# Attention and a gated MLP on one core: a sixth W1 buffer, other loads of k, q and v, and scale vectors spread by VectorE

## The chip, the cores and the metric

The kernel runs on one core of a Trainium2 chip. The metric is the device time of one execution in microseconds (us), as the median of several runs. The core has a matrix engine (TensorE, PE in the profile; its weight loads are shown apart as PEld), a vector engine (VectorE, DVE), an activation engine (ScalarE, ACT), a general engine (GpSimd, POOL) and an engine that here only issues transfers (SyncE, SP). Each takes its own instructions in order and waits for the others on semaphores.

## The reference

For each of 8 batches there is grouped-query attention (16 query heads, 4 key/value heads, 384 positions, head size 64). Its output, as 384 x 1024 values `x`, goes through a residual block that mixes positions and then a residual MLP of width 4096.

```python
k = np.repeat(k, 4, axis=1); v = np.repeat(v, 4, axis=1)
scores = (1 / 8) * np.matmul(q, k.transpose(0, 1, 3, 2))
attn = np.exp(scores - max); attn = attn / attn.sum(-1)
x = np.matmul(attn, v)                  # heads side by side: 384 x 1024
a1 = alpha1 * x + beta1
tok = np.einsum('ts,bsd->btd', w_tok, a1)
u = x + lam * tok
a2 = alpha2 * u + beta2
ch = np.maximum(a2 @ w_ch1, 0.0) @ w_ch2
out = u + lam * ch
```

All inputs are float32 in HBM; the matrix products run in bf16. The vectors `alpha1`, `beta1`, `alpha2`, `beta2` and `lam` have 1024 entries, one for each model column.

## The kernel before

**Passes.** `main(b)` is the MLP of batch b, in two passes. The first pass makes the 32 hidden blocks (`nt`, 128 rows of W1 columns each): 8 matmuls of 384 columns for each block, line L414, into one of two PSUM banks (tag "mm"). Even blocks are moved out of PSUM by ScalarE (L422), odd ones by VectorE (L424), so the bank of an odd block must be emptied while the next even block is computed. The second pass makes the output from the resident W2, 6 groups of 32 matmuls of 512 columns, L447. W1 does not stay: it comes as 16 chunks of two blocks for every batch, by GpSimd's casting loads (`load_w1`, L134), into a ring of `RING` buffers; a buffer's next load is issued when PE has finished the chunk in it. W2 comes once, in 16 pieces (`load_w2`, L139), in the first batch's passes.

**Side work.** `side(b + 1)` is the attention and position mixing of the next batch, written in small pieces between the matmuls of `main(b)`. `main` yields after every half block; a dictionary gives the pieces that follow each yield. `us[0]` are the units of the first pass, `us[1]` those of the second. In the first batch the blocks 0 to 3 are made early, so the units 0 to 3 are their ends, and from unit 4 on a unit divisible by four lies in the middle of an even block. All five engines' orders are as written (`manual_schedule`); an engine never passes over an instruction that waits.

**The lead.** Batch 0 has no pass before it: `side(0)` runs alone, about the first 37 us. Its order is `add(scores, i)` for 18 groups, with the dictionary `at` giving what follows each: the transposes of k and q, `av`, `a1`, `tok` and `spread`. Each `scores` group fills a PSUM pair that ScalarE empties with one exponential (L226).

**The scale vectors.** `vecs` holds four vectors on all 128 partitions: `g1` = alpha1, `h1` = beta1 times lam, `al2` = alpha2, `lam_t` = lam. They start as rows of float32 in 32 partitions (`rows_f`); `split` cuts them into three bf16 parts (L532, L534, L540), and `spread` (L332, L334) sends them to all partitions by matmuls with a selection matrix, followed by a copy from PSUM. `g1` is spread in the lead (after the score groups 3 and 12); the other three are spread in the first batch's first pass, at the units 34 to 54.

**k, q and v.** k of batch b comes as two float32 loads on SP's queue (`load_k`, L96, two staging buffers `kst`) and is cast and doubled by four copies (`place_k`, L107): for batch 2 on, by GpSimd. q and v come by GpSimd's casting loads (L116, L111). `load_next(b + 2)` issues these four copies, four q loads and three v loads. For batch 2 it stands at the end of the first batch's first pass, for later batches in the second pass. k and q are turned by TensorE (`k_transpose`, `q_transpose`) for batches 0 and 1 and by DMA transposes on SP's queue (`flip_k`, `flip_q`) from batch 3 on; of batch 2, k and the first quarter of q go by DMA transpose, the other three quarters of q by TensorE at the units 16, 24 and 32 of batch 1's first pass.

Of the kernel before, what the change touches and what calls it, by code (L numbers as in the profile page):

```python
# [12 lines left out]
def kernel(  # L13
# [21 lines left out]
    nc = tc.nc  # L35
# [13 lines left out]
    P = 128  # L49
# [8 lines left out]
    RING = 5  # L58
# [16 lines left out]
    hT = const.tile([P, NNT, S], bf, tag="hT", name="hT")  # L75
    vecs = const.tile([P, 4, DM], f32, tag="vecs", name="vecs")
# [3 lines left out]
    kT = const.tile([P, NST, Hkv, P], bf, tag="kT", name="kT")  # L80
# [10 lines left out]

    def load_k(b, hs=(0, 2)):
        ks.setdefault(b, [])
        for h in hs:
            t = sb.tile([P, 2, NST, D], f32, tag="kst", name="kst", bufs=2)
            nc.sync.dma_start(out=t, in_=k[b, h:h + 2].rearrange("h (p st) d -> p h st d", st=NST))  # L96
            ks[b].append(t)

    def place_k(b, i, hs=(0, 1)):
        if b not in k2s:  # L100
            k2s[b] = sb.tile([P, NST, Hkv, 2, D], bf, tag="k2", name="k2", bufs=1)
        copies = [nc.gpsimd.tensor_copy] * 2
        if b == 1 or b == 0 == i:
            copies = (nc.vector.tensor_copy, nc.vector.tensor_copy if i else nc.scalar.copy)
        lo, hi = hs[0], hs[-1] + 1
        for a in range(2):
            copies[a](out=k2s[b][:, :, 2 * i + lo:2 * i + hi, a, :], in_=ks[b][i][:, lo:hi].rearrange("p h st d -> p st h d"))  # L107
# [5 lines left out]
    def load_q(b):  # L113
        qrs[b] = sb.tile([P, Hq, NST, D], bf, tag="q_raw", name="q_raw", bufs=1)
        for h in range(0, Hq, G):
            nc.gpsimd.dma_start(out=qrs[b][:, h:h + G], in_=q[b, h:h + G].rearrange("h (p st) d -> p h st d", st=NST))  # L116

    def flip_k(b):
        nc.sync.dma_start_transpose(out=kT.rearrange("p st h s -> p (st h) s"),
                                    in_=k2s[b].rearrange("p st h a d -> p (st h a d)"))  # L120
# [53 lines left out]
    def side(b):  # L174
# [14 lines left out]
        def k_transpose(h0, n=2, tag="tp"):  # L189
            ps = tp_ps([P, n * NST, P], tag)  # L190
            for i in range(n * NST):
                nc.tensor.matmul(out=ps[:, i, :], lhsT=k2s[b][:, i % NST, h0 + i // NST].rearrange("p a d -> p (a d)"),
                                 rhs=ident, is_transpose=True, start=(i == 0), stop=(i == n * NST - 1), skip_group_check=True)
            nc.vector.tensor_copy(out=kT[:, :, h0:h0 + n, :].rearrange("p st h s -> p h st s"),
                                  in_=ps.rearrange("p (h st) s -> p h st s", h=n))
# [13 lines left out]
        def scores(i, later=False):  # L209
            sc = bank([P, 2, 4, P], "sc", "sc") if first else three()  # L210
            k = 4 * i
            while k < 4 * i + 4:
                n = min(4 * i + 4, k - k % NST + NST) - k
                p, sk, st = k // (NST * NST), k // NST % NST, k % NST
                for hh in range(2):
                    r = slice(hh * D, (hh + 1) * D)
                    nc.tensor.matmul(out=sc[:, hh, k % 4:k % 4 + n], lhsT=kT[r, sk, 2 * p // G, :],  # L217
# [109 lines left out]
        def spread(ps_, vs, tag, eng="DVE"):  # L327
            n = len(ps_)
            ps = bank([P, 4, P], tag, "vec")
            w = vs[1] - vs[0]  # L330
            for i, p in enumerate(ps_):
                nc.tensor.matmul(out=ps[:, i * w:(i + 1) * w], lhsT=sel[:, p:p + 1].to_broadcast([P, P]),  # L332
                                 rhs=rows_b[:, vs[0] * P:vs[1] * P], start=True, stop=True)
            evac(eng)(out=vecs[:, vs[0]:vs[1], ps_[0] * P:(ps_[-1] + 1) * P].rearrange("p v (n d) -> p n v d", n=n),  # L334
                      in_=ps[:, :n * w].rearrange("p (n v) d -> p n v d", n=n))
# [16 lines left out]
        if not first:  # L352


            turns = {16 + 8 * i: [(q_transpose, 2 + 2 * i, 2, "three")] for i in range(3)} if b == 2 else {}
            if b == 1:
                turns = {4: [(split, 2, 4, 0)], 8: [(split, 2, 4, 1)], 12: [(k_transpose, 0)],
                         16: [(q_transpose, 0, 2, "av")], 20: [(k_transpose, 2)]}
                for i in range(3):
                    turns[24 + 4 * i] = [(q_transpose, 2 + 2 * i, 2, "av")]  # L360
                for i in range(4):
                    turns[34 + 4 * i] = [(spread, (2 * i, 2 * i + 1), (1, 3), "tp", "ACT")]
                for i in range(2):
                    turns[50 + 4 * i] = [(spread, range(4 * i, 4 * i + 4), (3, 4), "av", "ACT")]
# [13 lines left out]
              2: [(q_transpose, 2, 2, "av")], 3: [(warmup, 1), (spread, lower, (0, 1), "tp")],  # L378
              4: [(av, 0)], 5: [(a1, 0)], 6: [(av, 1), (k_transpose, 2, 2, "tp")],
# [3 lines left out]
              12: [(spread, upper, (0, 1), "av"), (a1, 2)], 13: [(tok, 0), (av, 4), (a1, 3)],  # L383
# [12 lines left out]
    def load_next(b):  # L396
        place_k(b, 0)
        place_k(b, 1)
# [4 lines left out]
    def main(b):  # L403
# [3 lines left out]
        for c in range(NCH):  # L407
# [27 lines left out]
            if b == 0 and c == NCH - 1:  # L435
                for i in range(RING):
                    load_w1(NCH + i)
                load_next(2)
# [20 lines left out]
    with tc.manual_schedule(engines=order):  # L459
# [11 lines left out]
        hTf = hT.rearrange("p n s -> p (n s)")  # L471
# [25 lines left out]
        load_row(2, moe_alpha2)  # L497
# [44 lines left out]

        def fill_h(p):
# [17 lines left out]
        load_k(1)  # L561
# [4 lines left out]
        for f in side(0):  # L566
            f()
        place_k(1, 0)
        place_k(1, 1)
        load_k(2)  # L570
        for b in range(B):
            us = side(b + 1) if b + 1 < B else ({}, {})
            moves = [(0, 1, flip_k, 2), (0, 1, flip_q, 2, 0, 2)] if b == 1 else []
            if 0 < b < B - 2:
                moves += [(1, 1, load_k, b + 2), (1, 2, load_next, b + 2), (1, 34, flip_k, b + 2), (1, 36, flip_q, b + 2, 0, 2),
# [39 lines left out]
```

The softmax here doesn't subtract the row's maximum and nothing guards it: scores larger than these inputs give would overflow.

## Time and profile before

| what | value |
|---|---|
| median of 5 runs | 803.92 us (803.0 to 804.14) |
| profiled execution: its own time | 803.92 us |
| profiled execution: span of the program's instructions | 802.1 us |
| PE busy | 794.8 us, 99% of the span |
| DVE, ACT, POOL busy | 344.7, 226.5, 181.9 us |
| granted TensorE clock | 1.00 |
| one first pass, from batch 2 on | about 41.6 us |
| one second pass | about 55.0 us |
| DMA moved | 112.58 MB, mean 140 GB/s |

The profile is that of one execution. The span runs from the first to the last instruction of the program; 1.8 us of the execution's time lie outside it. A busy PE is not necessarily a PE at its peak, since matmuls are pipelined and their ends are modelled; the distance from one matmul's start to the next tells more.

### The profile page before, as it was taken

The numbers are of one execution on the slowest core, as the hardware profiler recorded it, in microseconds if no ns is written. First come the engines' busy times: TensorE is split into PE (matmuls) and PEld (weight loads), VectorE is DVE, ScalarE is ACT, GpSimd is POOL, SyncE is SP. The second block draws the span as 40 slices with busy tenths as digits, with TensorE's granted clock in tenths as the row PEclk, the third lists the DMA queues.
The fourth block names the chain that finished last, engine by engine and source line by source line (L and its number), as shares of the span: only waits on it lengthen the run. The fifth ranks groups of instructions, "written<-read, shape, count | busy, mean of one in ns | idle before, by whom it ended". The sixth has DMA issues, their size and how long they took to land.

```text
span 802.1 us, 14253 instructions
## 1 busy us (share of the span) xinstructions
PE 794.8 (99%) x6141; PEld 453.7 (57%) x6141; DVE 344.7 (43%) x667; ACT 226.5 (28%) x308; POOL 181.9 (23%) x241
## 2 busy tenths in 40 slices
PE   8999999999999999999999999999999999999997
PEld 4765555655556555565555655566555655556545
DVE  7652565316542256323662235622365225552122
ACT  7624331232412243123221234122431223312100
POOL 9234231341013500135002340033300330003000
PEclk9999999999999999999999999999999999999999
DMA  9999999999279962999339991499914994139611
GB/s 190 203 194 202 204 207 161 193 197 133 63 139 181 198 95 62 171 190 195 64 84 162 193 192 42 96 172 198 162 47 114 174 196 83 47 65 183 83 40 40
DMA packets 232575, 112.58 MB, mean 140 GB/s; under 512 B 81976, under 2 KB 226368, under 8 KB 232512
## 3 DMA queue, kind: packets, MB, share of 16 engines
q0 software_dynamic: 170752, 83.47, 79.0%
q1 hardware_dynamic: 61216, 27.81, 13.8%
q8 instruction: 48, 0.79, 0.4%
q10 hardware_dynamic: 544, 0.39, 0.2%
q14 instruction: 15, 0.12, 0.0%
HBM read 170.53 MB, written 12.58 MB: 228 GB/s over the span
## 4 chain that ended last, share of the span: by engine, by line
PE 86%; DMA 9%; issue 3%; DVE 1%; POOL 1%; ACT 0%; POOLq 0%
PE ch L447 37%; PE h L414 36%; DMA w<-in_moe_w_ch_dram 9%; PE sc L217 4%; PE sc L252 3%; PE sc L275 3%; POOL w L134 1%; PE h L168 1%; PE tok L275 0%; PE av L252 0%; PE warm L464 0%; PE tp L203 0%; PE ut L292 0%; DVE hT L534 0%; PE tok L279 0%
## 5 line engine op out<-in xcount | busy, mean ns | idle before, releaser
L447 PE MATMUL ch<-w,hT 128*128 128x512 bf16 (+2 forms) x1600 | 357.6, 371 | 0.9 <-DVE o L452 0.9
L414 PE MATMUL h<-a2T,w 128*128 128x384 bf16 (+1 forms) x2016 | 331.9, 326 | 0.2 <-DMA w<-in_moe_w_ch_dram 0.2
L414 PEld LDWEIGHTS <-w 128*128 128x128 bf16 x2016 | 196.5, 98 | 130.3 <-DMA w<-in_moe_w_ch_dram 1.4
L134 POOL DMA_DIRECT2D w<-in_moe_w_ch_dram x128 | 112.2, 877 | 525.7 <-PE h L414 507.0
L447 PEld LDWEIGHTS <-hT 128*128 128x128 bf16 x1600 | 144.7, 98 | 152.6 <-issue 10.1
L226 ACT ACTIVATE es<-sc 128x1024 bf16<-128x1024 f32 x126 | 121.4, 1023 | 187.7 <-PE sc L217 178.8
L424 DVE TENSOR_SCALAR hT<-h,bias 128x384 bf16<-128x384 f32 x128 | 79.1, 618 | 215.7 <-PE h L414 215.1
L422 ACT ACTIVATE hT<-h,bias 128x384 bf16<-128x384 f32 x128 | 74.3, 580 | 304.4 <-PE h L414 303.8
L452 DVE TENSOR_TENSOR o<-ch,vecs 128x512 f32<-128x512 f32 (+2 forms) x50 | 33.4, 669 | 107.9 <-PE ch L447 107.9
L252 PEld LDWEIGHTS <-es 128*128 128x128 bf16 x1008 | 38.3, 97 | 13.2
L275 PEld LDWEIGHTS <-wtokT 128*128 128x128 bf16 x576 | 37.4, 98 | 12.3 <-DVE a L265 1.7
L217 PE MATMUL sc<-qT,kT 64*128 64x384 bf16 (+2 forms) x576 | 42.1, 272 | 0.2
L252 PE MATMUL sc<-v,es 128*128 128x65 bf16 x1008 | 39.8, 193 | 0.0
L257 DVE RECIPROCAL rinv<-sc 128x6 f32<-128x6 f32 x56 | 10.8, 192 | 67.3 <-PE sc L252 66.7
L282 DVE TENSOR_TENSOR x<-sc,x 128x384 f32<-128x384 f32 x56 | 30.9, 552 | 20.0 <-PE sc L275 20.0
L275 PE MATMUL sc<-a,wtokT 128*128 128x128 bf16 x504 | 37.3, 219 | 0.0
L217 PEld LDWEIGHTS <-kT 64*128 64x128 bf16 x576 | 21.6, 94 | 24.0 <-issue 18.6
L453 DVE TENSOR_TENSOR o<-o,x 128x512 f32<-128x512 f32 (+2 forms) x50 | 33.5, 670 | 1.7
L286 DVE TENSOR_TENSOR a<-x,vecs 128x384 bf16<-128x384 f32 x56 | 32.6, 582 | 1.9
L263 DVE TENSOR_TENSOR a1f<-x,vecs 128x384 f32<-128x384 f32 x56 | 31.2, 557 | 1.9
L265 DVE TENSOR_TENSOR a<-a1f,vecs 128x384 bf16<-128x384 f32 x56 | 31.2, 557 | 1.9
L258 DVE TENSOR_TENSOR x<-sc,rinv 128x384 f32<-128x384 f32 x56 | 31.2, 557 | 1.9
(80 smaller groups left out, 211.8 us busy)
## 6 DMA issues: line engine op xcount, KB each, us to landing
w<-in_moe_w_ch_dram POOLq DMA_DIRECT2D x144, 512.0 KB, 8.9
out_dram<-o SPq DMA_DIRECT2D x47, 256.0 KB, 2.2
q_raw<-in_q_dram POOLq DMA_DIRECT2D x28, 192.0 KB, 8.6
kst<-in_k_dram SPq DMA_DIRECT2D x16, 192.0 KB, 3.7
v<-in_v_dram POOLq DMA_DIRECT2D x24, 64.0 KB, 8.3
a2T<-a SPq DMA_TRANSPOSE x56, 2.3
qg<-in_q_dram POOLq DMA_DIRECT2D x3, 192.0 KB, 4.6
stage<-in_q_dram ACTq DMA_DIRECT2D x2, 192.0 KB, 3.6
```

Source lines behind the costliest of these rows:

```text
L134: nc.gpsimd.dma_start(out=t, in_=w1src[:, :, c * CW * P:(c + 1) * CW * P])
L217: nc.tensor.matmul(out=sc[:, hh, k % 4:k % 4 + n], lhsT=kT[r, sk, 2 * p // G, :], rhs=qT[r, p, st:st + n, :], start=True, stop=True)
L226: nc.scalar.activation(out=e, in_=sc, func=EXP, scale=scale_qk)
L252: nc.tensor.matmul(out=av[:, hh, sq, :], lhsT=ess[k // 4][:, m % 2, k % 4, :], rhs=vb[:, sk, hk, :], start=(sk == 0), stop=(sk == NST - 1))
L275: nc.tensor.matmul(out=ps[:, tt, :], lhsT=wtokT[:, st, tt * P:(tt + 1) * P], rhs=a1s[p][:, st, :], start=(st == 0), stop=(st == NST - 1 an ...
L286: nc.vector.tensor_tensor(out=a2s[p], in0=u, in1=bc(al2, p), op=MUL)
L414: nc.tensor.matmul(out=ps[:, :n], lhsT=w1[:, dt, j * P:(j + 1) * P], rhs=a2T[:, dt, :n], start=(dt == 0), stop=(dt == NDT - 1))
L422: nc.scalar.activation(out=hT[:, nt, :], in_=ps[:, :S], func=RELU, bias=c1)
L424: nc.vector.tensor_scalar(out=hT[:, nt, :], in0=ps[:, :S], scalar1=c1, scalar2=0.0, op0=ADD, op1=mybir.AluOpType.max)
L447: nc.tensor.matmul(out=ps[:, lo:hi], lhsT=hT[:, nt, ms * P:(ms + 1) * P], rhs=w2[:, nt, dw * 512 + lo:dw * 512 + hi], start=(nt == 0), sto ...
L452: nc.vector.tensor_tensor(out=o[:, lo:hi], in0=ps[:, lo:hi], in1=lam_t[:, c], op=MUL)
L453: nc.vector.tensor_tensor(out=o[:, lo:hi], in0=o[:, lo:hi], in1=x[:, ms, c], op=ADD)
```

## The change

`RING` goes from 5 to 6, and the two pieces of code that depend on it move with it: the prologue loads six W1 chunks before q and v of batch 1, and the W2 loads of the first pass start one chunk earlier.

k of batch 2 and later comes by two casting loads on GpSimd's queue, straight into `k2` in both copies; SP's loads, the staging buffers and GpSimd's copies for these batches are gone. k of batches 0 and 1 is still staged, in a free part of `hT`. `k2` and `kT` have another layout, with the table `BLK` telling which block holds which third of the positions; the number and size of the matmuls stay.

At the end of the first batch's first pass only k of batch 2 is loaded. Its q is loaded in four pieces after the chunks 1 to 4 of batch 1's first pass, and its v after chunk 10. All four quarters of this q are turned by TensorE, at the units 24, 32, 40 and 48.

`spread` is left for `g1` alone, and its first half stands after score group 5 instead of 3. The other three vectors are loaded as rows of 512 entries into partitions 0, 32, 64 and 96 of three tiles (cleared by GpSimd first), and one VectorE stream shuffle for each half sends partition 0 of each group of 32 to the whole group. Two shuffles stand at each of the units 4, 12 and 20 of the first batch's first pass, each pair after the other's rows are loaded anew; `h1` is made by one product at unit 16. The transposes of batch 1 move to the units 8 and 24 to 40. k of batch 1 is loaded after the fourth piece of `side(0)`.

```diff
-    RING = 5
+    RING = 6
...
     def load_k(b, hs=(0, 2)):
+        if b > 1:
+            k_tile(b)
+            for a in range(2):
+                nc.gpsimd.dma_start(out=k2s[b][:, :, a], in_=by_head(k[b]))
+            return
         for h in hs:
-            t = sb.tile([P, 2, NST, D], f32, tag="kst", name="kst", bufs=2)
-            nc.sync.dma_start(out=t, in_=k[b, h:h + 2].rearrange("h (p st) d -> p h st d", st=NST))
+            ks[b, h // 2] = t = hTf[:, 7680 + 384 * h:8448 + 384 * h].bitcast(f32).rearrange(
+                "p (h st d) -> p h st d", h=2, st=NST)
+            nc.sync.dma_start(out=t, in_=by_head(k[b, h:h + 2]))
...
-            turns = {16 + 8 * i: [(q_transpose, 2 + 2 * i, 2, "three")] for i in range(3)} if b == 2 else {}
+            turns = {24 + 8 * i: [(q_transpose, 2 * i, 2, "three")] for i in range(4)} if b == 2 else {}
             if b == 1:
-                turns = {4: [(split, 2, 4, 0)], 8: [(split, 2, 4, 1)], 12: [(k_transpose, 0)],
-                         16: [(q_transpose, 0, 2, "av")], 20: [(k_transpose, 2)]}
+                turns = {4: [(to_all, 3, 0, 0), (to_all, 3, 1, 1), (load_row_set, 1, 1, 0), (load_row_set, 2, 0, 1)],
+                         8: [(k_transpose, 0)], 12: [(to_all, 1, 0, 2), (to_all, 1, 1, 0), (load_row_set, 2, 1, 0)],
+                         16: [(scale_beta,)], 20: [(to_all, 2, 0, 1), (to_all, 2, 1, 0)],
+                         24: [(q_transpose, 0, 2, "av")], 28: [(k_transpose, 2)]}
                 for i in range(3):
-                    turns[24 + 4 * i] = [(q_transpose, 2 + 2 * i, 2, "av")]
-                for i in range(4):
-                    turns[34 + 4 * i] = [(spread, (2 * i, 2 * i + 1), (1, 3), "tp", "ACT")]
-                for i in range(2):
-                    turns[50 + 4 * i] = [(spread, range(4 * i, 4 * i + 4), (3, 4), "av", "ACT")]
+                    turns[32 + 4 * i] = [(q_transpose, 2 + 2 * i, 2, "av")]
...
-              2: [(q_transpose, 2, 2, "av")], 3: [(warmup, 1), (spread, lower, (0, 1), "tp")],
-              4: [(av, 0)], 5: [(a1, 0)], 6: [(av, 1), (k_transpose, 2, 2, "tp")],
+              2: [(q_transpose, 2, 2, "av")], 3: [(warmup, 1)],
+              4: [(av, 0)], 5: [(spread, lower, "tp"), (a1, 0)], 6: [(av, 1), (k_transpose, 2, 2, "tp")],
...
     def load_next(b):
-        place_k(b, 0)
-        place_k(b, 1)
+        load_k(b)
...
             if b == 0 and c == NCH - 1:
                 for i in range(RING):
                     load_w1(NCH + i)
-                load_next(2)
+                load_k(2)
+            if b == 1 and c in range(1, 5):
+                load_q(2, [G * (c - 1)])
+            if b == 1 and c == NCH - RING:
+                load_v(2)
...
+        def load_row_set(i, half, place):
+            ap = (moe_alpha1, moe_beta1, moe_alpha2, moe_lam)[i]
+            nc.sync.dma_start(out=rows4[place][0:P:32],
+                              in_=bass.AP(tensor=ap.tensor, offset=ap.offset + half * 512, ap=[[0, 4], [1, 512]]))
+
+        def to_all(i, half, place):
+            nc.vector.stream_shuffle(out=vecs[:, i, half * 512:(half + 1) * 512], in_=rows4[place], mask=[0] * 32)
+
+        def scale_beta():
+            nc.vector.tensor_tensor(out=h1, in0=h1, in1=lam_t, op=MUL)
...
-        load_k(1)
         load_q(1)
         load_v(1)
         for i in range(3):
             load_w2(0, i, 8)
-        for f in side(0):
+        for i, f in enumerate(side(0)):
             f()
+            if i == 3:
+                load_k(1)
+        for i in range(3):
+            rows4.append(sb.tile([P, 512], f32, tag="es", name="rows4", bufs=EB))
+            nc.gpsimd.memset(rows4[i], 0.0)
+            load_row_set(*((3, 0), (3, 1), (1, 0))[i], i)
         place_k(1, 0)
         place_k(1, 1)
-        load_k(2)
...
-            moves = [(0, 1, flip_k, 2), (0, 1, flip_q, 2, 0, 2)] if b == 1 else []
+            moves = [(0, 1, flip_k, 2)] if b == 1 else []
             if 0 < b < B - 2:
-                moves += [(1, 1, load_k, b + 2), (1, 2, load_next, b + 2), (1, 34, flip_k, b + 2), (1, 36, flip_q, b + 2, 0, 2),
+                moves += [(1, 2, load_next, b + 2), (1, 34, flip_k, b + 2), (1, 36, flip_q, b + 2, 0, 2),
```

## The prediction

> **What bounds the kernel now.** I read the page's slices first, then the waits of PE, then the table by pass, and last the timelines of the two places that the change touches.
>
> ```profile
> PE   8999999999999999999999999999999999999997
> PEclk9999999999999999999999999999999999999999
> DMA  9999999999279962999339991499914994139611
> ```
>
> PE is busy in every slice at a full granted clock; the DMA engines are full only up to about 190 us and then in each first pass. The waits of PE (total us, times, longest):
>
> ```profile
> PE vec L332 <- DVE hT L540: 0.8, 1, 0.8
> PE h L414 <- DMA w<-in_moe_w_ch_dram: 0.2, 1, 0.2
> ```
>
> The passes, cut at their first matmuls (length, then busy time of PE, PEld, DVE, ACT, POOL, clock, DMA share, GB/s):
>
> ```profile
> 37.69:77.61 39.92, 39.92 (x278) 25.16 (x277) 16.40 (x41) 15.11 (x38) 16.50 (x21) 1.00 1.38 201
> 132.65:175.84 43.19, 42.95 (x276) 25.71 (x274) 12.32 (x20) 9.28 (x16) 13.12 (x15) 1.00 1.31 181
> 175.84:230.88 55.04, 55.04 (x481) 29.45 (x480) 30.46 (x59) 17.34 (x18) 7.88 (x12) 1.00 0.65 107
> 230.88:272.48 41.60, 41.60 (x257) 25.05 (x256) 10.65 (x17) 9.30 (x16) 13.12 (x15) 1.00 1.32 186
> ```
>
> A first pass of 256 matmuls takes 41.60 us, 0.1625 us a matmul, and every later one takes the same: there PE streams without a gap, and nothing in this change shortens it. So only three stretches can move: the lead (0 to 37.7), batch 0's first pass (39.92) and batch 1's first pass (43.19, where three transposes of 0.34 explain 1.02 and 0.57 is left over as stall). The span is 802.1 us, the profiled execution's own time 803.92, equal to the median; I carry the 1.8 us outside the span over unchanged.
>
> **Spreading by matmul goes, in batch 0's first pass.** The timeline shows six visits of `spread`; from the start of one to the next h matmul is 0.22 us (59.95 to 60.17, 71.28 to 71.50). No wait there, and PE is the bound, so 6 x 0.22 = 1.3 us go in full. The transposes only change places. ScalarE's six copies and VectorE's `split` go too; neither held PE up. **-1.3.**
>
> **One more q transpose in batch 1's first pass.** Four calls instead of three, 0.34 us each by the chain ("46.68 0.34 PE tp L203 x6"): **+0.34**. SP's first flip of q (136.30) goes; nothing waited for it.
>
> **The sixth buffer and W1 in batch 1's first pass.**
>
> ```profile
> 152.11 10.63 DMA w<-in_moe_w_ch_dram
> 162.78 13.22 PE h L414 x80
> ```
>
> This is the chain: a chunk issued at 152.11 lands 10.63 us later, and PE starts at once. With five buffers a chunk must land within four chunks of PE's work, 4 x 2.6 = 10.4 us, and the loads of this pass land 9.3 to 10.6 after issue: hence the stall. With six it is 5 x 2.6 = 13.0. Against that, four q loads come between: the same loads in batch 1's second pass land 1.0 apart (187.5, 188.5, 189.6, 190.6), so every chunk behind them is up to 4.2 later. But SP's float32 k (two loads at 137.9 and 138.6, 0.4 MB in all, 2 us at 198 GB/s) and the flip of q leave the start of the pass, where the first chunk took 9.3 rather than the 6.0 of batch 2's pass. So 7 to 9.3 + 4.2 = 11 to 13.5 against 13.0 and the transposes' extra 1.0: no stall, or 0.2. The first q piece, issued at about 5.3 + 0.9 us into the pass, lands after 12.6 to 15.5; its transpose stands in block 12, at 12 x 1.3 + 0.65 = 16.3. v is issued after chunk 10, behind every chunk that this pass needs. **-0.5** (0 to -0.57). A rule speaks against these loads. Their pieces in SBUF are 384 B long, and the Trainium skill (DMA: Bandwidth & Descriptors, Specifications) asks for at least 512 B at line rate; if that meant half the rate (an estimate), the four would cost 8.4 and a stall of some 3 us would follow. The row says otherwise: 192 KB in 1.0 us is 190 GB/s, where W1 with its longer pieces has 198 (512 KB in 2.65).
>
> **W1 and W2 in batch 0's first pass.** The order on GpSimd's queue moves chunk 5 before q and v of batch 1, but the sum ahead of chunk 6 (lands at 48.1) is the same, and SP's k of batch 2 (0.4 MB at 36 to 43) leaves the stretch: landings about 2 us earlier, PE about 1 us earlier. W2 gains the same 2 us. Zero, with that cover; without it PE would wait up to 1.
>
> **The k loads of later batches** go behind W1 on GpSimd's queue: 2 x 1.0 us more before q and v, which land by 192 + 2 where the flips stand at 216 and later. SP loses two loads and GpSimd four copies (1.85 us) that nobody waited for. Zero; if k came later than 216, SP's flips and outputs behind it would slip, but there are 25 us of room.
>
> **The lead.** The 0.8 us wait at L332 looks like a gain, but see what else ends there:
>
> ```profile
> 10.34 0.54 DVE L205 COPY qT<-tp 128x768 bf16<-128x768 bf16 x1
> 10.79 0.42 PE L217 MATMUL sc<-qT,kT 64*128 64x256 bf16 x4
> 11.25 7.57 ACT L226 ACTIVATE hT<-sc 128x1024 bf16<-128x1024 f32 x8 [0.49 <-PE sc L217]
> ```
>
> Score group 4 needs the q copy that ends at 10.88 on VectorE, so its second half starts at 10.93 with or without `spread` ahead: the exponentials start again at 11.2 either way. What does change is VectorE's order: the copy of `spread` (0.69 busy, 0.57 to the next start) moves from a moment when VectorE would idle to behind the first normalisation at 12.7, and pushes the following work by 0.57. The copies of k and q at 14.11 and 14.57 then end at 15.7; score group 9 needs them and started at 15.38; the third W_tok transpose, which waited for VectorE already (0.21), slips from 16.60 to about 17.1; score group 12 from 18.98 to about 19.4. ACT's exponentials give back little, since from 19 us PE is the bound. I take **+0.4**; bounds -0.3 (part of the 0.8 comes through) and +0.6 (the whole copy).
>
> **The rows and shuffles.** No shuffle is in the trace. The nearest row is VectorE's 128x512 float32 (L452, 669 ns), the bounds the 0.47 of L534 and the 1.02 of a copy that met GpSimd; I take 0.67, 0.6 start to start. The Trainium skill (VectorE: DVE Perf Modes, The perf-mode tier table) has shuffles at one element a cycle, about 2400 ns for 2048; by it 512 would take 0.6, and the sum would be the same.
>
> ```profile
> 39.28 0.62 DVE L424 TENSOR_SCALAR hT<-h,bias 128x384 bf16<-128x384 f32 x1
> 39.81 0.27 DVE L532 CAST hT<-hT 32x256 bf16<-32x256 f32 x1
> 40.70 0.62 DVE L424 TENSOR_SCALAR hT<-h,bias 128x384 bf16<-128x384 f32 x1
> ```
>
> The shuffles of unit 4 take the place of the line at 39.81: 39.81, 40.4, then block 5's bias copy at 41.0 and its activation from 41.2 to 41.8. Block 7 wants that bank at 41.77: 0.1 late at best. All this holds if the rows are there. They wait for GpSimd's clears, which stand behind the last early W2 load, which waits for the transfer eight places ahead (in before: issued 30.82, after a landing at 30.54); with chunk 5 in front that is 33.2. Three clears of about 0.65 (estimate from 0.23 for 128x128 and 0.12 for 128x32) put lam's second half on SP's queue at 35.4. The prologue's row loads landed 3.8 to 4.0 after issue, SP's k at 36.0 took 6.0 with the engines full: so 39.4 to 41.4 against 40.7 (40.4 plus the lead's shift). The next two pairs have 5.2 us each for a load that the pair before releases; at 4 to 5 nobody waits. While VectorE waits, the activation of every odd block is queued behind, and PE behind that. **+0.3**, from 0.1 to 2.7 with all loads at 6.0. `scale_beta` (two rows of 0.6) fits before block 11. GpSimd's clears delay only a W1 load that waits for PE until 37.8.
>
> **Sum.** -1.3 + 0.34 - 0.5 + 0.4 + 0.3 = -0.8: the span 801.3, the time 803.92 - 0.8 = **803.1 us**.
>
> **Rivals.** *Better:* the lead gives 0.3 of its wait and the rows are in time (0.1): -1.3 + 0.34 - 0.57 - 0.3 + 0.1 = -1.7, 802.2. For it: the wait at L332 is PE's longest after the start; against it: the q copy at 10.88. 24%. *Slower:* row loads at 6.0. Lam's second half at 41.4 to 42 makes block 7 wait 1.2, the pair at unit 12 adds little, that at unit 20 1.4, since each load is released later: 2.7 in place of 0.3, so -0.8 + 2.4 = +1.6, 805.5. It decides from 41 us on as the landing of lam. 13%. *W1 still late:* without the relief from SP's k, chunks land 14.5 after issue against 13.0 to 13.5: +1.3 for the -0.5, hence +1.0, 804.9. 8%. *Nothing reaches the end:* the matmuls removed only expose W1 or the bank waits in batch 0's pass: 803.9 to 804.4. 5%. The forecast has 50%.
>
> **How the numbers follow.** The forecast itself runs from 802.4 (lead 0, rows 0.1) to 804.0. The range 801.7 to 805.4 takes in the better case, the late W1 and most of the slow one, and leaves out 15 to 20%. About 0.2%, 1.6 us, is what a measurement of this kernel can tell from no change. Faster than 802.3: most of the better case and the low edge of the forecast, 0.27. Slower than 805.5: half of the slow case, some of the late W1 and what I do not see, 0.15. Between: 0.58.
>
> **What would show it.** Batch 0's first pass 38.6 to 39 us instead of 39.92, without L332 visits; batch 1's 42.9 to 43.0 with no wait for W1; later passes at 41.60 and 55.04 unchanged. In the lead, the first exponential after the fourth near 11.2, score group 12 later than 18.98, and the first pass starting at 37.7 to 38.2. A lead that ends before 37.5 makes the lead's term wrong; VectorE idle before a shuffle for more than 0.5 makes the rows' term wrong; a PE wait for W1 in batch 1 the buffer's.

## The result, and the profile after

The changed kernel takes **802.20 us** (median of 29 runs, 801.13 to 803.08) against 803.68 (49 runs, 802.48 to 804.68) for the kernel before, measured beside it: a ratio of 0.998, 95% interval 0.9974 to 0.9985. A second measurement, in a later session, gave 802.31 against 803.66, 0.9982 (0.9974 to 0.9991). On the medians the kernel became faster by 1.35 to 1.5 us, where 0.8 was forecast; the ratios say 1.45 to 1.6. The time lies inside the stated range of 801.7 to 805.4, and 0.2 below the forecast's own 802.4 to 804.0. The profiled execution took 802.04 us, its span is 800.3 us.

The slices of the page first, in tenths of busy time. Nothing has changed at this scale: PE is busy everywhere, and the page gives the full granted clock (more on its first microseconds below).

```profile
PE   8999999999999999999999999999999999999997
PEclk9999999999999999999999999999999999999999
DMA  9999999999279963999439992499914994139311
```

The waits of PE (total us, times, longest) show what came and went:

```profile
PE h L424 <- DVE hT L434: 0.2, 1, 0.2
PE h L424 <- DMA w<-in_moe_w_ch_dram: 0.2, 1, 0.2
```

The wait of `spread` in the lead (0.8 us before) is gone. A wait of an h matmul for VectorE's activation is new; it belongs to the shuffles. The wait for a W1 chunk is there as before, sixth buffer or not. The passes, cut at their first matmuls:

```profile
36.51:75.48 38.97, 38.77 (x262) 23.85 (x261) 19.95 (x49) 11.60 (x32) 15.44 (x19) 1.00 1.39 201
130.52:174.09 43.57, 43.35 (x281) 26.15 (x280) 12.88 (x21) 9.28 (x16) 18.41 (x22) 1.00 1.34 177
229.14:270.74 41.60, 41.60 (x257) 25.05 (x256) 10.65 (x17) 9.30 (x16) 13.12 (x15) 1.00 1.31 180
```

Against before: the lead ends at 36.51 instead of 37.69, batch 0's first pass is 38.97 instead of 39.92, batch 1's first pass 43.57 instead of 43.19, all others are the same to 0.01, and what follows the start of the last pass is 46.30 instead of 46.37. By this one pair of traces the lead gave 1.2 us, batch 0's pass 0.95, and batch 1's pass took 0.4 back. The experiments show that the first and the last of these numbers, and 0.37 of the second, change from one execution of the same kernel to the next.

### The profile page after: what moved, and what is told of

The parts are those of the page before. It is cut to its first block, busy times and chain, and to the rows that moved or that the text cites. A ratio compares the mean times of both kernels' runs of the same rounds, so it can differ in the third digit from the quotient of the medians.

```text
span 800.3 us, 14229 instructions
## 1 busy us (share of the span) xinstructions
PE 793.2 (99%) x6131; PEld 452.4 (57%) x6131; DVE 347.4 (43%) x676; ACT 222.8 (28%) x302; POOL 181.3 (23%) x232
## 4 chain that ended last, share of the span: by engine, by line
PE 93%; DMA 4%; POOL 2%; issue 1%; DVE 0%; POOLq 0%; DVEq 0%
PE ch L461 42%; PE h L424 39%; PE sc L232 4%; PE sc L267 4%; PE sc L290 4%; DMA q_raw<-in_q_dram 2%; DMA w<-in_moe_w_ch_dram 2%; POOL w L149 1%; DMA rows<-in_moe_lam_dram 1%; POOL v L125 0%; PE tp L218 0%; POOL qg L518 0%; DVE vecs L565 0%; POOL hT L550 0%; DVE o L466 0%
## 5 line engine op out<-in xcount | busy, mean ns | idle before, releaser
L434 DVE TENSOR_SCALAR hT<-h,bias 128x384 bf16<-128x384 f32 x128 | 79.1, 618 | 215.0 <-PE h L424 214.5
L290 PEld LDWEIGHTS <-wtokT 128*128 128x128 bf16 x576 | 37.4, 98 | 12.3 <-DVE a L280 1.7
L290 PE MATMUL sc<-a,wtokT 128*128 128x128 bf16 x504 | 37.3, 219 | 0.0
## 6 DMA issues: line engine op xcount, KB each, us to landing
q_raw<-in_q_dram POOLq DMA_DIRECT2D x28, 192.0 KB, 11.2
```

The costliest lines, as they stand in the source:

```text
L290: nc.tensor.matmul(out=ps[:, tt, :], lhsT=wtokT[:, st, tt * P:(tt + 1) * P], rhs=a1s[p][:, st, :], start=(st == 0), stop=(st == NST - 1 an ...
L434: nc.vector.tensor_scalar(out=hT[:, nt, :], in0=ps[:, :S], scalar1=c1, scalar2=0.0, op0=ADD, op1=mybir.AluOpType.max)
```

## The experiments

Four theories about the difference to the forecast were at stake: that the move of `spread` shortens the lead; that the lead's length is drawn anew in each execution; that the rows come late and cost the first pass something; and that batch 2's q loads take from W1 what the sixth buffer gives.

**The kernel before, once more, for a second trace.**

> The kernel before, unchanged, for a second trace of its lead. In the first trace the float32 transposes at 4.8 us stood 0.21 us apart, in the changed kernel's 0.11, and everything behind them was 0.4 to 0.7 us earlier there. Chance theory: how long PE runs at half its pace at the start differs between executions of one kernel; then this trace can show either, and a lead that ends anywhere from 36.5 to 37.7. Cause theory: the changed kernel's start is faster by itself; then this trace again has 0.21 at 4.8 us and a lead that ends at 37.5 to 37.9.

One execution of 803.84 us, span 802.06. Its lead ends at 37.31 instead of 37.69, batch 1's first pass is 43.40 instead of 43.19. The wait at `spread`, 0.8 us in the first trace, is 0.5 here:

```profile
PE vec L332 <- DVE hT L540: 0.5, 1, 0.5
```

So the same instructions differ by 0.4 us in the lead and 0.2 in that pass, and a pair of single traces can't settle terms of this size.

**The move of the lower `spread`, alone, in the kernel before.**

```diff
-              2: [(q_transpose, 2, 2, "av")], 3: [(warmup, 1), (spread, lower, (0, 1), "tp")],
-              4: [(av, 0)], 5: [(a1, 0)], 6: [(av, 1), (k_transpose, 2, 2, "tp")],
+              2: [(q_transpose, 2, 2, "av")], 3: [(warmup, 1)],
+              4: [(av, 0)], 5: [(spread, lower, (0, 1), "tp"), (a1, 0)], 6: [(av, 1), (k_transpose, 2, 2, "tp")],
```

> The kernel before with one edit: the lower half of the scale spread stands after score group 5 instead of 3. The prediction's step (VectorE's copy of it comes at a worse moment): lead 0.4 longer, time +0.4 us. Rival (the wait of PE at L332 did hold the lead up, and goes): lead 0.6 to 0.9 shorter, time -0.6 to -0.9. Chance theory (the lead's gain lies in the execution's start): no difference of the medians, within 0.2.

803.61 us (11 runs) against 803.29: ratio 1.0002 (0.9993 to 1.0011). The trace shows a lead of 36.60, 1.1 us shorter than that of before, and batch 0's first pass as it was:

```profile
36.60:76.52 39.92, 39.92 (x279) 25.16 (x276) 16.41 (x41) 15.15 (x38) 16.53 (x21) 1.00 1.39 204
```

Yet the median did not fall. A short lead in one trace is not a shorter kernel.

**The same move taken back, in the changed kernel.**

```diff
-              2: [(q_transpose, 2, 2, "av")], 3: [(warmup, 1)],
-              4: [(av, 0)], 5: [(spread, lower, "tp"), (a1, 0)], 6: [(av, 1), (k_transpose, 2, 2, "tp")],
+              2: [(q_transpose, 2, 2, "av")], 3: [(warmup, 1), (spread, lower, "tp")],
+              4: [(av, 0)], 5: [(a1, 0)], 6: [(av, 1), (k_transpose, 2, 2, "tp")],
```

> The changed kernel with the same piece put back: spread after score group 3. Against the changed kernel (-1.5 us to before): by the prediction's step 0.4 faster, -1.9; by the rival 0.6 to 0.9 slower, -0.6 to -0.9; by the chance theory the same, -1.5.

801.63 (10 runs) against 803.29: 0.9979 (0.9969 to 0.9988). Without the move the changed kernel is at least as fast, lead 36.78. Batch 0's first pass is 38.60 here, batch 1's 43.19.

**The changed kernel once more.**

> The changed kernel once more, for a second trace and a time beside the three kernels that follow. Theory A (the lead's length is drawn anew in each execution: 36.5 to 36.8 us when VectorE's three-way split of the rows ends before GpSimd's copies of k, 37.3 to 37.7 us when the two meet): the lead of this trace is one of these two kinds, with the split's second product at 0.3 to 0.4 us in the first kind and at 0.5 us or more in the second; the median is 802.0 to 802.4. Theory B (the short lead belongs to the changed kernel itself): the lead is 36.5 to 36.6 again, whatever the split took. Under both, batch 0's first pass is 38.6 to 39.0, batch 1's 43.0 to 43.6.

802.31 (11 runs) against 803.66. Theory A holds: with the same code as the 36.51 above, this trace's lead ends at 37.68. The passes, in the same columns:

```profile
37.68:76.27 38.59, 38.59 (x261) 23.84 (x260) 19.77 (x49) 11.60 (x32) 16.18 (x20) 1.00 1.39 201
131.32:174.67 43.35, 43.16 (x281) 26.14 (x280) 12.87 (x21) 9.29 (x16) 18.41 (x22) 1.00 1.34 178
```

Here are the two kinds of lead side by side: PE's six float32 transposes of q, VectorE's second product of the three-way split of the rows, and the copy of q that score group 4 needs. First the short lead (the changed kernel's first trace, 36.51), PE and VectorE:

```profile
4.77 1.16 PE L218 MATMUL tp<-hT,stage 128*128 128x128 f32 x6
```

```profile
8.14 0.34 DVE L547 SCALAR_TENSOR_TENSOR hT<-hT,stage 32x128 f32<-32x128 bf16 x1
8.66 0.54 DVE L220 COPY qT<-tp 128x768 bf16<-128x768 bf16 x1
```

Then the long one (its second trace, 37.68):

```profile
4.82 1.56 PE L218 MATMUL tp<-hT,stage 128*128 128x128 f32 x6
10.53 0.29 PE L232 MATMUL sc<-qT,kT 64*128 64x256 bf16 x2 [0.47 <-DVE qT L220]
```

```profile
8.99 0.58 DVE L547 SCALAR_TENSOR_TENSOR hT<-hT,stage 32x128 f32<-32x128 bf16 x1
9.94 0.54 DVE L220 COPY qT<-tp 128x768 bf16<-128x768 bf16 x1
```

PE does the same six transposes in 1.16 us here and in 1.56 there; over all traces it is 1.16 to 1.45 us with a short lead and 1.54 to 1.56 with a long one. In the long case VectorE comes to the product 0.85 us later, the product itself takes 0.58 instead of 0.34, and the q copy is late enough that group 4's second half waits for it. All traces are of one kind or the other: the second product starts at 8.1 to 8.5 and the lead ends at 36.5 to 36.8 (seven traces, one of them of the kernel before with the move alone), or it starts at 8.99 or 9.00 and the lead ends at 37.3 to 37.7 (seven traces, both of the unchanged kernel before among them; of that kernel no trace has the short lead).

What differs behind this is the moment at which PE's pace doubles. Up to 4.0 us the warm-up matmuls (128 x 384) start 0.32 us apart in every trace, after the first record of a granted clock of 1.00 in the trace those of the same shape start 0.16 apart. This first record comes at 4.6 to 6.0 us in the seven traces with the short lead and at 6.2 to 7.5 in the seven with the long one (4.7 in the changed kernel's first trace and 6.6 in its second; 6.9 in both of the kernel before, 5.1 with the move alone). Where there is no record, a view of the profile gives 1.00 too, so the clock column says 1.00 from 3 to 8 us in both kinds; the pace of the matmuls tells more. Three warm-up matmuls in the changed kernel's first trace, after its first clock record, and the same three in the trace of the last experiment below, where the first record comes at 7.5 us:

```profile
6.19 0.66 PE L478 MATMUL warm<-wtokT 128*128 128x384 bf16 x3
```

```profile
6.86 0.98 PE L478 MATMUL warm<-wtokT 128*128 128x384 bf16 x3
```

So the kind of lead goes with how long PE runs at half its pace in the execution, as the chance theory of the second trace had it, and not with the code. No run sets this moment, so that it makes the lead long is read from the order of the fourteen traces; what sets it is not shown.

**GpSimd's last two k copies of batch 0 behind its scaled rows.** In the long leads the split's second product runs beside the copies, which start at 8.84 us; if that meeting made the long lead, this edit should make it rarer.

```diff
         load_w1(1)
-        place_k(0, 1)
         scale_rows(1, nc.gpsimd)
+        place_k(0, 1)
         split(1, 2, None, nc.gpsimd)
```

> The changed kernel with GpSimd's two copies of k (batch 0) behind its scaling of a row instead of ahead. The traces so far show two kinds of lead: VectorE's last row step is short (0.34 us) and ends before 8.9 where it runs ahead of GpSimd's copies (8.84 to 9.87), and takes 0.58 to 1.02 and ends at 9.6 to 10.0 where it meets them; the leads end at 36.5 to 36.8 and 37.3 to 37.7. If meeting GpSimd's copies is the cause: no meeting at 8.9 to 9.4, the step is 0.34 to 0.4 in nearly every execution, the lead 36.4 to 36.8, and the median -0.4 to -0.6 against the changed kernel (-2.0 to before). If the start of VectorE's chain alone decides (PE's pace at 4.8 us): the same spread of times as the changed kernel, -1.5 to before.

802.01 (11 runs, 801.23 to 802.88) against 803.71: 0.998 (0.9972 to 0.9989), no different from the changed kernel. Its trace has a short lead (36.70), which agreed with the theory; the last experiment below has the same exchange and a long one, so the theory falls. Their first clock records, at 5.0 and 7.5 us, fit the two leads.

**Lam's second shuffle at unit 8**, since the first trace showed VectorE waiting for a row.

```diff
-                turns = {4: [(to_all, 3, 0, 0), (to_all, 3, 1, 1), (load_row_set, 1, 1, 0), (load_row_set, 2, 0, 1)],
-                         8: [(k_transpose, 0)], 12: [(to_all, 1, 0, 2), (to_all, 1, 1, 0), (load_row_set, 2, 1, 0)],
+                turns = {4: [(to_all, 3, 0, 0), (load_row_set, 1, 1, 0)],
+                         8: [(k_transpose, 0), (to_all, 3, 1, 1), (load_row_set, 2, 0, 1)], 12: [(to_all, 1, 0, 2), (to_all, 1, 1, 0), (load_row_set, 2, 1, 0)],
```

> The changed kernel with the second shuffle of lam behind the k transposes of unit 8 instead of beside the first at unit 4. In the changed kernel's trace the pair waited 0.24 us for its rows and block 7 waited 0.37 for its bank; with the spread moved back it waited for nothing. If the pair is what holds the bank: the first batch's first pass is 38.60 in the trace, and the time 0 to 0.4 better than the changed kernel's (-1.5 to -1.9 to before). If the rows' landing is the cause and not the pair: the pass stays at 38.9 or more, no gain.

801.91 (9 runs) against 803.71: 0.9976 (0.9967 to 0.9986). Batch 0's first pass is 38.60. That alone doesn't speak for parting the pair: the lead is 36.83 here, and with the pair together and leads of 36.70 and 36.78 (the exchange and the move taken back) the pass is 38.60 too. What speaks for it is the pass of 38.60 behind a lead of 36.54 in the kernel with both edits further down, where the pair is apart, beside 38.97 and 38.78 behind 36.51 and 36.52 with the pair together. The time is 0.3 below the changed kernel's own median, within what the runs vary.

What the late row did is in VectorE's timeline, first trace of the changed kernel:

```profile
38.95 0.01 DVE L565 LOAD_MASK_SELECT vecs<-rows  x1 [0.24 <-DMA rows<-in_moe_lam_dram]
38.98 0.73 DVE L565 STREAM_SHUFFLE vecs<-rows 128x512 f32<-128x512 f32 x1
39.65 0.73 DVE L565 STREAM_SHUFFLE vecs<-rows 128x512 f32<-128x512 f32 x1
40.45 0.62 DVE L434 TENSOR_SCALAR hT<-h,bias 128x384 bf16<-128x384 f32 x1
```

and in the second trace, whose lead was 1.17 us longer:

```profile
39.81 0.73 DVE L565 STREAM_SHUFFLE vecs<-rows 128x512 f32<-128x512 f32 x1
40.44 0.73 DVE L565 STREAM_SHUFFLE vecs<-rows 128x512 f32<-128x512 f32 x1
41.23 0.62 DVE L434 TENSOR_SCALAR hT<-h,bias 128x384 bf16<-128x384 f32 x1
```

In the first, VectorE was free 0.24 us before the rows came (issued at 34.39, there at 38.85), the activation of the line with L434 ended at 41.08, and block 7 began at 41.13 where it could have begun at 40.76: the 0.37 us between 38.60 and 38.97. With the long lead the rows are in time and nothing waits. So in this trace the row wait eats a third of what the short lead brings.

**Five W1 buffers in the changed kernel.**

```diff
-    RING = 6
+    RING = 5
```

> The changed kernel with five W1 buffers instead of six (the W2 loads and q's and v's place follow by their formulas). Chunks landed up to 14.1 us after issue in batch 1's first pass; with five buffers they have 10.4 us. If the sixth buffer pays for the q loads: that pass grows from 43.57 by up to 2.6 to 46.2, and the time is +1.1 to before instead of -1.5. If it does nothing there (the stall is set by the rate of the DMA engines): the pass stays at 43.6 to 44.2, and the time within 0.5 of the changed kernel's.

805.49 (11 runs) against 803.29: 1.0022 (1.0013 to 1.0031). The waits of PE and batch 1's first pass:

```profile
PE h L424 <- DMA w<-in_moe_w_ch_dram: 2.4, 3, 0.9
```

```profile
131.61:177.72 46.11, 43.63 (x281) 26.06 (x280) 12.88 (x21) 9.30 (x16) 18.46 (x22) 1.00 1.35 178
```

Three waits instead of one, and a pass 2.5 to 2.8 us longer than in the changed kernel's traces (43.57, 43.35). Batch 0's second pass is 0.28 longer as well, 55.32, with a wait of 0.2 for W2. The sixth buffer pays for the q loads that now lie in this pass. Without it the whole change would be a loss of 2.2 us against the kernel before on the medians, 1.8 by the ratio.

**Batch 2's q and v loaded at the end of batch 0's first pass**, as before the change, so that W1 has batch 1's first pass to itself.

```diff
-                load_k(2)
-            if b == 1 and c in range(1, 5):
-                load_q(2, [G * (c - 1)])
-            if b == 1 and c == NCH - RING:
-                load_v(2)
+                load_next(2)
```

> The changed kernel with q and v of batch 2 loaded behind its k at the end of the first batch's first pass, as in the kernel before, instead of inside batch 1's first pass. Crowding theory (the q loads inside the pass make W1 late, 13 to 14 us to landing): W1 lands in about 10 us again, under the 13.0 of six buffers, and that pass is 42.96 (41.60 and four transposes) instead of 43.2 to 43.6: time -0.3 to -0.6 against the changed kernel, about -2.0 to before. Rate theory (the DMA engines are the bound up to 190 us wherever the loads stand): the first chunks of that pass come later, and the pass stays at 43.2 or more: -1.5 to before.

803.16 (11 runs) against 803.71: 0.9998 (0.9989 to 1.0006). W1 now lands 7 to 9 us after its issue and PE never waits for it, yet most of the change's gain is gone. None of the theories had said what the waits and the chain of this trace show:

```profile
PE h L424 <- DMA a2T<-a: 1.4, 2, 1.1
```

```profile
126.75 6.37 DMA a2T<-a
133.16 2.92 PE h L424 x17
```

`a2T`, the operand of the first pass, is made by DMA transposes on SP's queue. Where little else is loaded such a transpose lands 2.3 us after its issue (most of those in later batches whose landing was recorded, both kernels). Here q and v of batch 2 are still coming (q from 132.3 us, v until 138.4), the last transpose takes 6.37, and batch 1's first pass starts at 130.34, stops twice and is 44.61 long. In the changed kernel only W1 and k are loaded before the pass; the last of k lands at 130.61, and the pass, begun at 130.52, doesn't stop. In the kernel before, a chunk of W1 and the two loads of k fewer stood ahead of q and v on GpSimd's queue (W1's last early chunk landed at 124.9, here at 127.9, and k here at 130.5); q had landed by 129.8 and the last transpose took 3.52, just in time. No run tells the chunk's share from that of k. So in the changed kernel, moving q and v into batch 1's first pass is worth 0.8 to 0.9 us on the medians (0.55 below before with the early loads, 1.35 to 1.48 without) and 1.3 to 1.45 by the ratios; the two differ since the eleven times with the early loads fall into two groups and the median is at the edge of one. The pass itself is 1.0 to 1.3 longer than in the changed kernel's traces. The reason is `a2T`, and not W1's arrival.

**The early loads, the shuffles apart, and q's first quarter by DMA transpose, as before the change.**

```diff
-            turns = {24 + 8 * i: [(q_transpose, 2 * i, 2, "three")] for i in range(4)} if b == 2 else {}
+            turns = {16 + 8 * i: [(q_transpose, 2 + 2 * i, 2, "three")] for i in range(3)} if b == 2 else {}
...
-            moves = [(0, 1, flip_k, 2)] if b == 1 else []
+            moves = [(0, 1, flip_k, 2), (0, 1, flip_q, 2, 0, 2)] if b == 1 else []
```

(with the edits of the two experiments on the shuffles and on the early loads)

> A version that should beat both: the changed kernel with q and v of batch 2 loaded early, the shuffles of lam apart, and the first quarter of batch 2's q turned by a DMA transpose as in the kernel before (three transposes in batch 1's first pass instead of four). If the three costs add: passes 38.60 and 42.62, -0.4 and -0.9 against the changed trace, time about -2.5 to before. If the DMA transpose takes the DMA engines from W1 at the start of the pass, as it did before: that pass 43.0 or more, time about -2.0.

802.80 (11 runs) against 803.71: 0.9992 (0.9983 to 1.0001). Batch 1's first pass is 44.68, with one transpose call less and two waits for `a2T` again (1.8 us together, 1.4 before); the early loads cost here at least what they cost alone.

**The move taken back and the shuffles apart, together; then q's loads spaced; then GpSimd's exchange too.** The three kernels add one edit each. Spaced loads:

```diff
-            if b == 1 and c in range(1, 5):
-                load_q(2, [G * (c - 1)])
+            if b == 1 and c in (0, 2, 4, 6):
+                load_q(2, [G * (c // 2)])
```

> The changed kernel with the lower spread back behind score group 3 and lam's second shuffle at unit 8. If what each gave alone (0.2 to 0.6 us of the median) is real and they add, the median is 801.3 to 801.6, 0.6 to 0.9 below the changed kernel; if the two were only the spread of the runs, it is 801.9 to 802.3. Batch 0's first pass 38.6, batch 1's 43.0 to 43.5, a W1 wait of PE of at most 0.4 there.

> The kernel before this one in the list, with batch 2's four q loads behind the chunks 0, 2, 4 and 6 of batch 1's first pass instead of 1 to 4. Theory A (each q load pushes every W1 chunk behind it by its own 1.0 us, and the chunk issued after chunk 4 has three of them ahead): that chunk has one or two fewer ahead and lands 12 to 12.7 us after its issue instead of 13.5 to 14.1, so that PE's wait for it goes; q's first quarter lands 3 us earlier, so that its transposes wait for nothing; batch 1's first pass is 42.9 to 43.1, and the time 0.1 to 0.4 below the kernel with the loads at 1 to 4. Theory B (the slow stretch of the DMA engines at 136 to 146 us is a matter of place and not of these loads): W1 lands 13.5 or later all the same and the pass stays at 43.0 to 43.6.

> The same once more, with GpSimd's scaled rows ahead of its last two k copies of batch 0, so that these copies come after VectorE's split. Theory A (the two kinds of lead come from the meeting of these copies with the split): the lead is 36.5 to 36.8 in the trace, the median 0.2 to 0.5 below the kernel without the exchange, 801.0 to 801.4, and its runs lie closer together. Theory B (the meeting is a sign of a slow start and not its cause): lead of either kind, median the same within 0.2.

| kernel (same chip) | us, runs | ratio to before (interval) | lead ends | batch 0's, batch 1's first pass | W1 from issue to landing, longest of the first six |
|---|---|---|---|---|---|
| before | 803.66, 24 | | | | |
| changed, again | 802.31, 11 | 0.9982 (0.9974 to 0.9991) | 37.68 | 38.59, 43.35 | 13.9 |
| move back, shuffles apart | 801.91, 8 | 0.9978 (0.9968 to 0.9988) | 36.54 | 38.60, 42.94 | 12.9 |
| and q spaced | 801.83, 8 | 0.9974 (0.9964 to 0.9985) | 37.30 | 38.60, 42.94 | 11.2 |
| and GpSimd's exchange | 801.66, 8 | 0.9971 (0.9961 to 0.9981) | 37.38 | 38.60, 42.94 | 10.9 |

The passes of the last one:

```profile
37.38:75.98 38.60, 38.60 (x262) 23.91 (x260) 19.95 (x49) 11.61 (x32) 16.06 (x20) 1.00 1.39 201
131.03:173.97 42.94, 42.94 (x282) 26.37 (x280) 12.88 (x21) 9.28 (x16) 18.41 (x22) 1.00 1.35 179
```

Spacing does to W1 what its first theory said and a little more: the slowest of the early chunks takes 11.2 us, 1.7 less, where 12 to 12.7 was expected. Chunks later in these passes take up to 13.0 and are in time; PE is busy through the whole pass. But the kernel before it in the list already had a pass of 42.94 in its trace, and the two medians differ by 0.08: the gain in time isn't shown. The last kernel has the lowest median of all, 2.0 us below before. It beats the kernel before; that it beats the changed kernel isn't shown, since the two intervals overlap.

Its lead is a long one with the exchange in place: the split's second product takes 0.55 at 8.99 us, beside GpSimd's scaled rows, and begins before the k copies, which come from 9.26 on. Keeping the copies away doesn't prevent the long lead.

The two kinds of lead can be read from the times as well. The eight of the last kernel are 800.85 to 801.16 (three) and 801.54 to 801.90 (five), its profiled one, with the long lead, is 801.90. The eleven of the kernel with the early loads are 802.88 to 803.16 (six) and 804.00 to 804.08 (five); its profiled one, with the short lead, is 802.89. The medians of the two groups lie 0.84 apart where `spread` stands after group 3, where the traces have leads of 36.5 to 36.8 and 37.3 to 37.4, and 1.13 apart where it stands after group 5, where they have 36.5 to 36.8 and 37.7. That the two groups of times are the two kinds of lead is an inference: only the profiled executions have a trace. The 49 times of the kernel before, 802.48 to 804.68, show no such gap.

## Why the prediction came out as it did

The direction was right and the largest term exact. Of the smaller terms the rows' was too high, the lead's is seen in one kind of lead alone, and the step on W1 in batch 1's first pass failed, though its sum is not refuted. One effect was not seen.

**Spreading by matmul, -1.3: right.** Batch 0's first pass went from 39.92 to 38.59 or 38.60 in nine of the eleven traces with the change in this place, -1.32. With the move alone in the kernel before it stayed at 39.92. No run puts the matmuls back alone, but the count leaves little else: the pass has 262 of PE's matmuls instead of 278, 16 fewer, as many as the six visits had (2, 2, 2, 2, 4 and 4), and PE is busy throughout before (39.92 of 39.92) and after (38.59 of 38.59 in the second trace).

**The rows and shuffles, +0.3: too high.** The step's fear was rows that land at 39.4 to 41.4. Lam's first half was issued at 34.39 and landed 4.5 later; the second half was issued at 35.06, 0.3 before the forecast's 35.4, and was there when its shuffle began at 39.65. The three clears took 1.47 us together and not 1.95. The cost is 0.37 where a short lead makes PE early (0.2 in one other trace) and nothing elsewhere. The shuffle itself takes 0.72 to 0.73, 0.63 start to start at the least, against 0.67 and 0.6 in the text; the estimate of 0.6 worked out there from the Trainium skill's figure (VectorE: DVE Perf Modes, The perf-mode tier table) is 0.1 low for one instruction and near the 0.63. The slower rival, rows at 6.0 us after issue, did not occur.

**One more q transpose, +0.34, and the sixth buffer, -0.5.** Together -0.16, a pass of about 43.0. The changed kernel's two traces have 43.57 and 43.35, where the kernel before had 43.19 and 43.40: by these nothing is gained in sum. Four more traces have the changed kernel's loads in this pass, with 43.41, 43.19, 43.04 and 42.94, and one more has those of before, with 43.69; the means of all are 43.25 and 43.43, -0.2, so a gain of the forecast size is neither shown nor refuted. What failed is a step: the chunk's time from issue to landing, forecast at 11 to 13.5 us. This is the chain of the first trace:

```profile
146.59 14.06 DMA w<-in_moe_w_ch_dram
160.69 2.45 PE h L424 x14
```

Each q load delays all that follows by 1.03 to 1.06 us, as its row in batch 1's second pass had said, and four make 4.2. The first chunk landed 6.3 after its issue, better than the 7 to 9.3 forecast, but the second came 5.5 us behind it, about twice the 2.65 that a chunk needs at full rate, and so 9.7 after its own issue; from there the q loads lead to 14.06. In the kernel with both edits the second chunk came 4.55 after the first, the same loads landed in 12.9, and the pass was 42.94, exactly the sum of the step. Why this second chunk varies by 1 us between executions stays open. The 0.6 us that the first trace has above 42.96 are two waits, by the distances of the matmuls' starts: 0.4 for this chunk, and 0.2 for the first q piece, which landed at 146.92, 16.4 us into the pass, where the prediction had 12.6 to 15.5 and needed it at 16.3. The rival "W1 still late" (+1.0) forecast such landings (14.5) from a start without the relief; the first chunk had it (6.3 against 9.3 before), the second hardly (9.7 against 10.3), and the price was 0.4 to 0.6 in these two traces.

The rule weighed there, pieces of at least 512 B for line rate (the Trainium skill, DMA: Bandwidth & Descriptors, Specifications), doesn't show as half the rate here: 192 KB in 384 B pieces take 1.03 to 1.06 us more, 185 to 191 GB/s, against 198 for W1.

**The lead, +0.4: right in the long lead, absent in the short one.** VectorE's copies in the long lead of the changed kernel, with `spread` after group 5:

```profile
9.94 0.54 DVE L220 COPY qT<-tp 128x768 bf16<-128x768 bf16 x1
12.21 0.68 DVE L348 COPY vecs<-vec 128x512 f32<-128x512 f32 x1
14.10 0.55 DVE L210 COPY kT<-tp 128x768 bf16<-128x768 bf16 x1
14.56 0.55 DVE L220 COPY qT<-tp 128x768 bf16<-128x768 bf16 x1
```

and with `spread` after group 3 (q spaced, also a long lead):

```profile
9.94 0.54 DVE L220 COPY qT<-tp 128x768 bf16<-128x768 bf16 x1
10.51 0.69 DVE L348 COPY vecs<-vec 128x512 f32<-128x512 f32 x1
13.72 0.55 DVE L210 COPY kT<-tp 128x768 bf16<-128x768 bf16 x1
14.18 0.55 DVE L220 COPY qT<-tp 128x768 bf16<-128x768 bf16 x1
```

The q copy is at the same time in both; the copy of `spread` moves from an idle moment into a busy stretch, the k and q copies slip by 0.38, and the lead ends at 37.68 instead of 37.30. That is the step as written. What it did not know is that the profile of before showed only one kind of lead, at its longest (the second product took 1.02 there, the first clock record came at 6.9 us). In the short lead group 4 doesn't wait for the q copy, and the move costs nothing that these traces show. On the medians its price can't be told from nothing: ratio 1.0002 when it is made alone, and 0.2 to 0.3 us less when it is taken back, each against its own runs of before. The sign that the prediction set itself, "a lead that ends before 37.5 makes the lead's term wrong", came true in the first trace and meant nothing: the same code ends at 37.68 in the second. Two more of its signs failed in the same way: the first exponential after the fourth came at 10.86 in the long lead and 9.95 in the short one, not near 11.2, and score group 12 began at 18.98 in the long lead and 17.81 in the short one, no later than before. The better rival, 802.2, has the measured time by luck and not by its reason: the 0.3 that it wanted from the wait at `spread` don't come from the move.

**Zeros.** The k loads of later batches, W1 and W2 in batch 0's first pass: from batch 2 on the passes are 41.60 and 55.04 to 55.05 in every trace, and PE waits for no W1 in batch 0. Right. Not in the sum: the stretch from the last pass's start on is shorter by 0.07 or more in every trace of a changed kernel (46.22 to 46.30 against 46.37 and 46.38).

**The sum by what the traces hold:** -1.32 (spread) + 0 (rows) + 0.2 to -0.2 (batch 1's pass, by the two pairs and by all traces) - 0.07 (end) gives -1.2 to -1.6 without the lead, and the medians say -1.35 to -1.5. So the lead's share is within about 0.3 of nothing. The forecast's -0.8 missed by about the 0.3 for the rows and the 0.4 for the lead.

**Not seen at all:** that a sixth chunk and the loads of k ahead of q and v would hold back the DMA transposes of `a2T` if the loads stayed where they were. It was no term of the sum, since the change moves these loads too; but it is what the move of the loads is worth, while the prediction looked for its effect in W1 alone.

## What to carry to other kernels

A profile is one execution. Where the first microseconds fix how engines meet, a lead may come in two lengths, and a stall seen there may be a draw, not a property: take a second trace of the unchanged kernel, and compare the pace of its first matmuls, before pricing anything below a microsecond in it. A ring's extra buffer is worth what else is to share its queue: price it together with those loads, by what an operand has to wait for at each place where they could stand.

## What had not been expected

- The same six float32 transposes of PE at 4.8 us take 1.16 or 1.56 us in executions of the same code, and values between (1.21 to 1.45) in four of the other traces. The profile's clock column says 1.00 in all of them, since it counts the time before the first clock record as full; that record comes at 4.6 to 7.5 us, and the matmuls' pace doubles there.
- The split's products on VectorE, 32 x 128, take between 0.34 and 1.02 us. Those beside GpSimd's computing at 8.99 us took 0.55 to 1.02, but one of 0.68 lay beside GpSimd's issue of loads only, so GpSimd's computing isn't shown to be the whole cause.
- A DMA transpose of `a` lands 2.3 us after its issue where little else is loaded, and 5.7 to 8.2 us after beside GpSimd's queued casting loads in batch 0's second pass; in these traces it cost time only where the next pass began meanwhile.
